# A new order of the same work in an attention and expert kernel on one core

## The chip, the core and the metric

The kernel runs on one core of one Trainium2 chip. A core has TensorE (PE in the profile, with PEld for its loads of stationary operands), VectorE (DVE), ScalarE (ACT), GpSimd (POOL) and SyncE (SP, which only issues transfers). The metric is the device time of one execution in microseconds (us); lower is better.

## The reference

The inputs q, k and v have 8 batch entries, 8 heads, 576 positions and 64 numbers a head, in float32. The expert part has a gate vector of 512, w1 (512 x 1024), w2 (1024 x 512) and a capacity of 128.

```python
q_rot, k_rot = (rotate(q), rotate(k))            # rotary embedding, halves of 32
scores = 1/sqrt(D) * np.matmul(q_rot, k_rot.transpose(0, 1, 3, 2))
attn = np.exp(scores - scores.max(-1)); attn /= attn.sum(-1) + 1e-09
x = matmul(attn, v)  -> (B, S, 512)
scores = np.einsum('bsd,d->bs', x, w_gate)       # expert part, for each batch entry
top_idx = np.argpartition(-scores[b], capacity)[:capacity]
ye = np.maximum(x[b, top_idx] @ w1, 0.0) @ w2
out[b, top_idx] = x[b, top_idx] + sigmoid(scores[b, top_idx])[:, None] * ye
```

## The kernel before, in words

Four heads make a group; there are two groups for each batch entry and 16 in all. A group's four heads are two pairs, so pairs are numbered 0 to 31, and pairs 2g and 2g+1 belong to group g. For a pair, q and k come from memory as two planes (the numbers, and the numbers with their halves swapped) into the tiles q_in and k_in, of which four each are used in turn; `rotate` multiplies both planes by a table (tabk) and adds them. Pair 0 is cut in column pieces and its rotation is written for VectorE, the pieces of q after the first for VectorE or GpSimd (`both`). Pairs 1 to 3 may also go to either; pair 1 is multiplied plane by plane. All later pairs are rotated on GpSimd.

`attend` then works through nine units of 64 rows (`units`). A unit multiplies q by k for one pair or for both pairs ("scores") into banks of PSUM. There are eight banks and a unit takes two for each of its pairs. In groups 0 and 1 the first 6 and 3 units are done pair by pair (`APART`). A unit's scores leave their banks in one of two ways, chosen by the table `DRAINS` (one letter for group, pair and unit): "V" means that VectorE copies and finds the row's extreme in one instruction; "S" means that ScalarE copies and VectorE finds the extreme from the copy. ScalarE then takes the exponential with the row sum, and VectorE transposes blocks (`turn`, STREAM_TRANSPOSE). `value` multiplies the transposed rows (tile prob) by v (tile vt) in six steps of 96 multiplications into four banks, copies the result (ot), transposes it on TensorE and scales it by the row sums into x; `half_done` stores x and multiplies it by the gate vector on GpSimd (tile prod). After every second group `route` ranks the positions of a batch entry, `chosen` gathers the chosen rows back from memory (GpSimd, tile xe), and `experts_of` runs w1, relu (ht) and w2 and scatters the rows.

The order of the work is a table. Every `op` gets a number in the order in which the program makes it, and `LINES` lists for each engine the numbers in the order in which that engine shall run them, two characters each; an op that several engines could run goes to the one whose line lists it. `Order.run` plays these lines with assumed costs (`SWITCH` and `RESTART` for TensorE when it changes between its three kinds of work or begins after a wait, the two lines on `wire` and `lasts` for transfers), and gets from that one order over all engines and the PSUM banks of each op. The instructions are written out in that order; on the chip an engine runs its own in that sequence and waits on semaphores. The assumed costs are no instructions: they reach the chip only through the order and the banks. A transfer marked `alone` waits until the one three before it has landed (`DEPTH = 3`). Because ops are written through one helper, all instructions show line L243; rows are told apart by tile names.

Of the kernel before, what the change touches and what calls it, by code (L numbers as in the profile page):

```python
# [33 lines left out]
010Q0H1e151n0Y1w1D1s1i1J0U100L19352Z2P3h3a2U312K1T3o1U3v1V1W3B1X1Y3I5a5g5G2521235m5z5L5t5W5R3R3S3T3U3V3W6V6Q6+417c433-75  # L34
7o7v7h7B6566674B68696a4I6f6h9a8Y936j4L7L9h7M7N7O9m7P7Q9x9s9D7Z4O9J7V7X4SaC4TaPaI4VaW8n4Wb1b79T9Ubd9V9Wbk9X9Ybpc+cNa18ucU
d3a54Ya38x4Z4+da4-bAbBdfbCbDdkbEbFdvdpepbObKbM8AeveC8E8FeIdGeOdHeUdIdJdKdLeZgxdUdQccdS8H8If4fagDcj8K8LgIcm8MgO8Ng-gVfkfl
h5fmhbfnfofphgiacpfwfyfuimighrithshtiyhuhvhwiKiEiQhBhFhDctcukmiVkhfYcwcxkskzg3czkFcAkKcBg6kQcCj4j5kWj6j7j8j9l0lVjijgjeg9
# [6 lines left out]
7n71787r7A747b7u6b6c7D6g9e9b7F9094977T8Z99924Q6p8-969l9j9g9p9d9o7R7S9A6r9z9E9r4P9w7+9C9I9u9GaD854U9NaQaJ87aMaT9LaLa+aX4X
b49-b8aHaFaOb0bhb6b3beaVaZaSbgbj9+9ZbsbobacObccRcVbmd7brcQbud4a4a6d6bId2d0d9abcTcZdccXaddjdhde8CdobHbGdydmdqafduesds8Bez
dxdAbUeFewdO8GbWeJeBeEbYereReHeNeLeQeueyeWeYeTdNdMe+f1gAdVdTf0f38Jd+f5gCf7f9gHgzfefcgJcrgFgSgLgPh0gNgUgRgWh4e0h2h6g+hagY
hfhde2h8fqfrhhibhjhlcqiniqfEihidfGijifilipivixisiBhyhxiLiHiAiDiJiGhGcvhLkniWhNkriNiPiSiUcyktkAi+iYjckwkpklkjkHkCkLkTkykJ
kNkPkEkZkvkSkYkVk-jajbl2lWl4gahPmcgbmlmim8mgm0jom7mkmemrmam2lYjsmtl+m4mnmymqlhlgmClnmwmEmBo4gfmImHo8ocmKo3oeoagio6okowoq
# [1029 lines left out]
```

## Time and profile before

| | us |
|---|---|
| median of 3 runs (lowest, highest) | 521.37 (519.64, 522.71) |
| the profiled execution's own time | 518.34 |
| its span, first to last instruction | 516.6 |
| PE busy in the span | 484.8 (94%) |
| DVE busy | 449.5 (87%) |
| ACT busy | 392.0 (76%) |
| POOL busy | 349.9 (68%) |

The profiled execution lies below all three timed runs, so differences are worked out against it and then applied to the median. The 1.7 us between its span and its own time lie outside the first and last instruction. Busy time of PE counts modelled ends of pipelined matmuls; where matmuls follow one another, the distance between starts is the safer number.

### The profile page before, as it was taken

The page shows a single profiled execution, that of the slowest core. Times are in us where ns is not written, and L with a number is a line of the kernel's source. Part 1 is how long each engine was busy: PE and PEld are TensorE (multiplying, and loading weights), DVE is VectorE, ACT ScalarE, POOL GpSimd, SP SyncE. Part 2 cuts the span into 40 slices and gives each one's busy share as a digit, 9 for nine tenths or more (in the row PEclk, how much of TensorE's full clock was granted, in tenths as well). Part 3 has the DMA queues.
Part 4 walks back from the last instruction along what each step waited for, and adds up shares of the span by engine and source line. Part 5 has one row for each costly group of instructions (what it writes and reads, how often), then busy time and mean ns, then how long its engine had stood idle before and what let it go on. Part 6 is the DMA issues. An engine that isn't in the chain of part 4 may idle for free.

```text
span 516.6 us, 18965 instructions
## 1 busy us (share of the span) xinstructions
PE 484.8 (94%) x7988; PEld 303.3 (59%) x7988; DVE 449.5 (87%) x781; ACT 392.0 (76%) x1040; POOL 349.9 (68%) x304
## 2 busy tenths in 40 slices
PE   8679978799999999999999999999999998999995
PEld 7345545455665456664567555674658455666872
DVE  6899999999999999989989998999949998993710
ACT  1598999998889989987778868977579967981100
POOL 2977498699884997749797796947796588114110
PEclk9798999999999999999999999999999999999998
DMA  8776556565554737235651746460642543132210
GB/s 293 233 258 201 159 176 203 177 194 159 152 173 127 202 114 217 82 120 167 206 163 61 204 129 222 132 221 16 184 137 86 161 138 110 50 86 64 88 42 20
DMA packets 47381, 76.53 MB, mean 148 GB/s; under 512 B 4928, under 2 KB 28224, under 8 KB 47296
## 3 DMA queue, kind: packets, MB, share of 16 engines
q1 hardware_dynamic: 45472, 70.54, 45.0%
q0 software_dynamic: 1280, 4.20, 2.4%
q8 instruction: 63, 1.03, 0.9%
q10 hardware_dynamic: 544, 0.59, 0.4%
q14 instruction: 22, 0.18, 0.1%
HBM read 63.77 MB, written 11.53 MB: 146 GB/s over the span
## 4 chain that ended last, share of the span: by engine, by line
PE 42%; POOL 10%; issue 9%; ACT 6%; DVE 4%; DMA 3%; POOLq 0%; ACTq 0%; DVEq 0%; SPq 0%
PE banks L243 42%; POOL k_in L243 3%; POOL q_in L243 3%; ACT prob L243 3%; POOL prod L243 2%; DVE prob L243 2%; ACT ot L243 2%; DVE nm L243 1%; DMA q_in<-q_dram 1%; DMA k_in<-k_dram 1%; ACT prod L243 1%; DVE past L243 0%; POOL xe L243 0%; POOL out_dram L243 0%; ACT ht L243 0%
## 5 line engine op out<-in xcount | busy, mean ns | idle before, releaser
L243 ACT ACTIVATE prob<-prob,nm 128x576 f32<-128x576 f32 x288 | 220.7, 771 | 25.8 <-DVE prob L243 14.3
L243 PE MATMUL banks<-k_in,q_in 64*64 64x288 f32 x2304 | 181.9, 420 | 22.6 <-ACT prob L243 5.1
L243 DVE STREAM_TRANSPOSE prob<-prob 128x2304 f32<-128x2304 f32 (+2 forms) x98 | 187.1, 1926 | 3.7 <-ACT prob L243 3.5
L243 PE MATMUL banks<-prob,vt 32*64 32x288 f32 x4608 | 151.6, 405 | 0.0
L243 PEld LDWEIGHTS banks<-k_in,q_in 64*64 64x64 f32 x2304 | 86.8, 134 | 106.7 <-ACT prob L243 23.0
L243 PEld LDWEIGHTS banks<-prob,vt 32*64 32x64 f32 x4608 | 98.3, 132 | 50.0 <-issue 14.1
L243 DVE TENSOR_SCALAR_CACHE_REDUCE prob<-banks 128x576 f32<-128x576 f32 x142 | 103.9, 746 | 13.5 <-PE banks L243 10.5
L243 ACT ACTIVATE prob<-banks 128x576 f32<-128x576 f32 x146 | 92.2, 653 | 28.9 <-PE banks L243 28.4
L243 DVE TENSOR_REDUCE nm<-prob 128x1 f32<-128x576 f32 x146 | 103.6, 738 | 3.4 <-ACT prob L243 3.1
L243 POOL TENSOR_TENSOR q_in<-q_in,tabk 128x1152 f32<-128x1152 f32 (+1 forms) x32 | 82.3, 2578 | 14.8 <-DMA q_in<-q_dram 14.5
L243 POOL TENSOR_TENSOR k_in<-k_in,tabk 128x1152 f32<-128x1152 f32 (+1 forms) x31 | 81.5, 2630 | 10.8 <-DMA k_in<-k_dram 7.9
L243 POOL TENSOR_TENSOR prod<-x,wg 128x512 f32<-128x512 f32 (+1 forms) x45 | 49.5, 1099 | 30.4 <-DVE x L243 13.9
L243 PE MATMUL banks<-xt,w1t 128*128 128x128 f32 x512 | 61.5, 277 | 0.1
L243 PEld LDWEIGHTS banks<-xt,w1t 128*128 128x128 f32 x512 | 58.9, 192 | 4.2 <-issue 2.3
L243 PE MATMUL banks<-w2t,ht 128*128 128x512 f32 x128 | 60.9, 607 | 0.3 <-ACT ht L243 0.3
L243 ACT ACTIVATION_READ_ACCUMULATOR prob<-prob,nm 128x1 f32 x288 | 56.1, 195 | 0.0
L243 POOL TENSOR_SCALAR sel<-slots,rank 128x128 bf16<-128x128 bf16 x35 | 20.6, 608 | 40.0 <-DVE rank L243 40.0
L243 POOL TENSOR_TENSOR k_in<-k_in 128x576 f32<-128x576 f32 x31 | 44.5, 1437 | 0.8
L243 POOL TENSOR_TENSOR q_in<-q_in 128x576 f32<-128x576 f32 x30 | 42.6, 1425 | 0.4
L243 PEld LDWEIGHTS banks<-w2t,ht 128*128 128x128 f32 x128 | 22.3, 189 | 23.9 <-issue 23.5
L243 ACT ACTIVATE prod<-prod 128x256 f32<-128x256 f32 (+1 forms) x54 | 22.0, 411 | 8.5 <-POOL prod L243 8.4
L243 POOL DMA_INDIRECT out_dram<-xe,idx x8 | 8.3, 1040 | 29.6 <-DVE xe L243 28.8
(69 smaller groups left out, 284.4 us busy)
## 6 DMA issues: line engine op xcount, KB each, us to landing
k_in<-k_dram SPq DMA_DIRECT2D x64, 288.0 KB, 3.6
vt<-v_dram SPq DMA_DIRECT2D x96, 192.0 KB, 3.1
q_in<-q_dram SPq DMA_DIRECT2D x62, 288.0 KB, 3.4
out_dram<-x SPq DMA_DIRECT2D x32, 256.0 KB, 2.8
w2t<-w_dram SPq DMA_DIRECT2D x8, 256.0 KB, 4.0
w1t<-w_dram SPq DMA_DIRECT2D x8, 256.0 KB, 3.4
out_dram<-x SPq DMA_DIRECT2D x16, 64.0 KB, 2.6
tabk<-rope_dram ACTq DMA_DIRECT2D x2, 288.0 KB, 4.2
```

The source lines that it names most:

```text
L243: i = made(*args, **kwargs)
```

## The change

Three assumed costs change, and the two tables are made anew: `LINES` for all five engines, and `DRAINS`.

```diff
-RESTART = (70.0, 130.0, 70.0)
+RESTART = (70.0, 130.0, 130.0)
...
-                            wire = max(wire, begin + takes) + o.moved / 350.0
-                            lasts = max(wire - begin + 1700.0, takes + 1400.0 + o.moved / 137.0)
+                            wire = max(wire, begin + takes) + o.moved / 300.0
+                            lasts = max(wire - begin + 2200.0, takes + 1900.0 + o.moved / 137.0)
...
-            on = any_of(n) if both else {"DVE": dve(n)} if first else {"POOL": pool(n)}
+            on = {"DVE": dve(n) if first else dve(n, 1, 700.0), "POOL": pool(n)} if both else {"DVE": dve(n)} if first else {"POOL": pool(n)}
...
-        ("VVVVVSSSS", "SVSSSVSVS"),
-        ("SSVSSSSSV", "SVSSSSVSS"),
+        ("VVVVVVVVV", "VSVVVSSSV"),
+        ("SSSSSSSVV", "SSSVSVVSS"),
...
-0B0D0E0F2G2H2I2E2J2F2C2D521-545356555857593Z6O6I2a6P6J6K6M6L6N2c8Q6d2e8S484a8U4c8T8R8W8X4C8VaA4Kay6oaB6qau4Navaw6saxaz82
+0B0z0C0D0F0E0G2C2A2D2B2y2w2z2x1V514Z4+4X4Y4-50526H6I246D6E6F6G3S266B6C8I28668J8M8K418N43458O4v8P8Latan4Dao6h7L4Gar6jasau
```

The first: a unit of scores that begins behind a wait is assumed to cost 130 ns and not 70. The second: a transfer is assumed to run at a lower rate and to last 500 ns longer. The third: a rotation instruction of pairs 1 to 3 is assumed to take 700 ns longer on VectorE. No instruction changes its operands, but some change their engine: in the whole program 148 pieces of scores leave PSUM by "V" and 140 by "S" (before: 142 and 146), four of the sixteen relus go from ScalarE to VectorE, and four scalings of x from VectorE to ScalarE.

Three places of the new order follow. The first is GpSimd at the start of the program; k_in1 and q_in1 are pair 1, q_in0 is pair 0, the tiles with 2 and 3 are pairs 2 and 3 (group 1). A row with tabk is a multiplication, one without it a sum. Before:

```order
L243 TENSOR_TENSOR k_in1_79<-k_in1_79,tabk_69 128x576
L243 TENSOR_TENSOR k_in1_79<-k_in1_79 128x576
L243 TENSOR_TENSOR q_in1_75<-q_in1_75,tabk_69 128x576 x2
L243 TENSOR_TENSOR k_in3_81<-k_in3_81,tabk_69 128x1152
L243 TENSOR_TENSOR k_in3_81<-k_in3_81 128x576
L243 TENSOR_TENSOR q_in3_77<-q_in3_77,tabk_69 128x1152
```

Now:

```order
L243 TENSOR_TENSOR k_in1_79<-k_in1_79,tabk_69 128x576
L243 TENSOR_TENSOR q_in0_74<-q_in0_74,tabk_69 128x2x192
L243 TENSOR_TENSOR k_in1_79<-k_in1_79,tabk_69 128x576
L243 TENSOR_TENSOR k_in1_79<-k_in1_79 128x576
L243 TENSOR_TENSOR q_in1_75<-q_in1_75,tabk_69 128x576 x2
L243 TENSOR_TENSOR q_in1_75<-q_in1_75 128x576
L243 TENSOR_TENSOR q_in3_77<-q_in3_77,tabk_69 128x1152
L243 TENSOR_TENSOR k_in3_81<-k_in3_81,tabk_69 128x1152
```

GpSimd has taken over the other half of k_in1's multiplication, one multiplication of q_in0 and the sum of q_in1; pairs 2 and 3 come after these. VectorE in the same stretch, before (prob0 is group 0; TENSOR_SCALAR drains a unit by "V", TENSOR_REDUCE belongs to "S"):

```order
L243 TENSOR_SCALAR prob0_86,nm0_93<-banks_63 128x576
L243 STREAM_TRANSPOSE prob0_86<-prob0_86 128x576
L243 TENSOR_SCALAR prob0_86,nm0_93<-banks_63 128x576
L243 TENSOR_REDUCE nm0_93<-prob0_86 128x1
L243 TENSOR_TENSOR q_in1_75<-q_in1_75 128x576
L243 STREAM_TRANSPOSE prob0_86<-prob0_86 128x576 x3
L243 TENSOR_REDUCE nm0_93<-prob0_86 128x1
L243 TENSOR_SCALAR prob0_86,nm0_93<-banks_63 128x576
```

Now:

```order
L243 TENSOR_SCALAR prob0_86,nm0_93<-banks_63 128x576 x2
L243 TENSOR_TENSOR q_in0_74<-q_in0_74 128x192
L243 TENSOR_SCALAR prob0_86,nm0_93<-banks_63 128x576 x2
L243 STREAM_TRANSPOSE prob0_86<-prob0_86 128x576
L243 TENSOR_SCALAR prob0_86,nm0_93<-banks_63 128x576 x2
L243 STREAM_TRANSPOSE prob0_86<-prob0_86 128x576 x5
L243 TENSOR_SCALAR prob0_86,nm0_93<-banks_63 128x576
```

The sum of q_in1, which stood between a reduction and three transposes, is gone from VectorE, and the last sum of q_in0 (128x192) stands behind two drains and waits for GpSimd's multiplication.

The second place is TensorE in the expert part of batch entry 3 (minus, past: counting the rank; w2t, ht: the second expert product; tok, sel: the index; k_in, q_in: scores). Before:

```order
L243 MATMUL banks<-minus,past_115 128x1
L243 MATMUL banks<-w2t,ht_101 128x512 x2
L243 MATMUL banks<-k_in_78,q_in_74 64x288
L243 MATMUL banks<-k_in_79,q_in_75 64x288
L243 MATMUL banks<-k_in_78,q_in_74 64x288
L243 MATMUL banks<-k_in_79,q_in_75 64x288
L243 MATMUL banks<-k_in_78,q_in_74 64x288
L243 MATMUL banks<-k_in_79,q_in_75 64x288
L243 MATMUL banks<-k_in_78,q_in_74 64x288
L243 MATMUL banks<-k_in_79,q_in_75 64x288
L243 MATMUL banks<-w2t,ht_101 128x512 x4
L243 LDWEIGHTS sel_107
```

Now:

```order
L243 LDWEIGHTS past_115
L243 MATMUL banks<-minus,past_115 128x1
L243 MATMUL banks<-w2t,ht_101 128x512 x6
L243 LDWEIGHTS sel_107
L243 MATMUL banks<-tok_110,sel_107 128x5
L243 LDWEIGHTS sel_107
```

The unit of scores no longer stands between two runs of the expert product; it stands in a run of five units (40 multiplications) ahead of the counting. Over the whole program the runs of scores, of values and of other work fall from 168 to 157. From the first use of gathered rows on, runs of scores fall from 65 to 58 and runs of value products from 33 to 32, and the longest runs of scores there are five units where they were four.

The third place is GpSimd around the gather of batch entry 5 (out_5; rs, sums: the guard on the row sums; prod, x, wg: products with the gate vector). Before:

```order
L243 DMA xe1_103<-out_5_dram,idx1_109 128x512
L243 TENSOR_SCALAR rs1_96<-sums1_92 64x2x5 x2
L243 TENSOR_SCALAR rs1_96<-sums1_92 64x2x4 x2
L243 TENSOR_TENSOR q_in3_77<-q_in3_77,tabk_69 128x1152
L243 TENSOR_TENSOR q_in2_76<-q_in2_76,tabk_69 128x1152
L243 TENSOR_TENSOR q_in3_77<-q_in3_77 128x576
L243 TENSOR_TENSOR q_in2_76<-q_in2_76 128x576
L243 TENSOR_TENSOR k_in3_81<-k_in3_81,tabk_69 128x1152
L243 TENSOR_TENSOR k_in3_81<-k_in3_81 128x576
L243 TENSOR_TENSOR prod0_97<-x0_89,wg_70 64x256
L243 TENSOR_TENSOR k_in2_80<-k_in2_80,tabk_69 128x1152
L243 TENSOR_TENSOR k_in2_80<-k_in2_80 128x576
```

Now:

```order
L243 DMA xe1_103<-out_5_dram,idx1_109 128x512
L243 TENSOR_TENSOR prod0_97<-x0_89,wg_70 128x512
L243 TENSOR_TENSOR q_in3_77<-q_in3_77,tabk_69 128x1152
L243 TENSOR_TENSOR prod0_97<-x0_89,wg_70 128x512
L243 TENSOR_TENSOR k_in3_81<-k_in3_81,tabk_69 128x1152
L243 TENSOR_TENSOR q_in3_77<-q_in3_77 128x576
L243 TENSOR_TENSOR k_in3_81<-k_in3_81 128x576
L243 TENSOR_TENSOR prod0_97<-x0_89,wg_70 64x256
L243 TENSOR_TENSOR q_in2_76<-q_in2_76,tabk_69 128x1152
L243 TENSOR_TENSOR k_in2_80<-k_in2_80,tabk_69 128x1152
L243 TENSOR_TENSOR k_in2_80<-k_in2_80 128x576
L243 TENSOR_TENSOR q_in2_76<-q_in2_76 128x576
```

The guard on the sums is gone to ScalarE, and two large products of x now stand ahead of and between the multiplications of pairs held in the tiles 2 and 3.

## Rows read from the trace of the kernel before

**Rows 1.** Page, part 1: busy us (share of the span) and instructions, by engine.

```profile
PE 484.8 (94%) x7988; PEld 303.3 (59%) x7988; DVE 449.5 (87%) x781; ACT 392.0 (76%) x1040; POOL 349.9 (68%) x304
```

**Rows 2.** Stretch, length; busy PE, PEld, DVE, ACT, POOL; granted clock; DMA share, GB/s.

```profile
0.00:20.00 20.00, 14.03 (x94) 11.25 (x94) 16.06 (x41) 5.94 (x12) 10.82 (x18) 0.97 0.84 278
20.00:40.00 20.00, 16.66 (x142) 9.17 (x146) 17.83 (x29) 16.53 (x38) 15.79 (x8) 0.84 0.78 242
40.00:60.00 20.00, 19.59 (x400) 11.12 (x396) 18.91 (x29) 18.54 (x43) 14.41 (x11) 0.93 0.51 153
60.00:120.00 60.00, 49.42 (x1017) 29.57 (x1012) 59.65 (x92) 59.07 (x173) 48.81 (x41) 1.00 0.66 198
120.00:480.00 360.00, 354.14 (x6163) 220.07 (x6156) 327.02 (x551) 289.30 (x772) 254.97 (x219) 1.00 0.46 137
```

**Rows 3.** Timeline of the start: begin, length, instruction, idle time before it.

```profile
10.39 0.75 DVE L243 TENSOR_TENSOR k_in<-k_in,tabk 128x576 f32<-128x576 f32 x1
10.56 1.85 POOL L243 TENSOR_TENSOR k_in<-k_in,tabk 128x576 f32<-128x576 f32 x1 [7.94 <-DMA k_in<-k_dram]
...
16.72 2.62 POOL L243 TENSOR_TENSOR k_in<-k_in,tabk 128x1152 f32<-128x1152 f32 x1
16.79 3.16 DVE L243 TENSOR_TENSOR q_in<-q_in 128x576 f32<-128x576 f32 x1
...
20.01 14.58 PE L243 MATMUL banks<-k_in,q_in 64*64 64x288 f32 x118 [4.40 <-DVE q_in L243]
...
22.94 0.75 DVE L243 TENSOR_REDUCE nm<-prob 128x1 f32<-128x576 f32 x1 [0.98 <-ACT prob L243]
...
36.56 0.74 DVE L243 TENSOR_SCALAR_CACHE_REDUCE prob<-banks 128x576 f32<-128x576 f32 x1
...
37.46 1.20 PE L243 MATMUL banks<-k_in,q_in 64*64 64x288 f32 x16 [2.87 <-POOL k_in L243]
```

**Rows 4.** Groups by line and shape: count, busy us, mean ns of one.

```profile
L243 DVE TENSOR_SCALAR_CACHE_REDUCE prob<-banks 128x576 f32<-128x576 f32 x142 | 103.9, 746 | 13.5 <-PE banks L243 10.5 <-ACT prod L243 1.5 <-ACT prob L243 0.5
L243 DVE TENSOR_REDUCE nm<-prob 128x1 f32<-128x576 f32 x146 | 103.6, 738 | 3.4 <-ACT prob L243 3.1
...
L243 ACT ACTIVATE prob<-banks 128x576 f32<-128x576 f32 x146 | 92.2, 653 | 28.9 <-PE banks L243 28.4
...
L243 POOL TENSOR_TENSOR k_in<-k_in,tabk 128x1152 f32<-128x1152 f32 x30 | 79.6, 2656 | 2.9 <-PE banks L243 2.7
...
L243 POOL TENSOR_TENSOR q_in<-q_in 128x576 f32<-128x576 f32 x30 | 42.6, 1425 | 0.4
L243 POOL TENSOR_TENSOR prod<-x,wg 128x512 f32<-128x512 f32 x30 | 38.5, 1283 | 26.0 <-DVE x L243 13.9 <-ACT prod L243 5.7 <-DMA k_in<-k_dram 3.2
...
L243 POOL TENSOR_TENSOR q_in<-q_in,tabk 128x576 f32<-128x576 f32 x2 | 2.8, 1404 | 0.0
```

**Rows 5.** Timeline of TensorE alone, later in the run.

```profile
414.66 1.71 PE L243 MATMUL banks<-prob,vt 32*64 32x288 f32 x48
416.30 1.20 PE L243 MATMUL banks<-k_in,q_in 64*64 64x288 f32 x16
417.43 3.17 PE L243 MATMUL banks<-prob,vt 32*64 32x288 f32 x96
420.53 1.20 PE L243 MATMUL banks<-k_in,q_in 64*64 64x288 f32 x16
421.66 2.68 PE L243 MATMUL banks<-prob,vt 32*64 32x288 f32 x80
```

**Rows 6.** Timeline around the gather of batch entry 5.

```profile
411.14 1.11 POOL L243 DMA_INDIRECT xe<-out_dram,idx  x1 [0.28 <-POOL idx L243]
...
415.64 0.86 POOL L243 TENSOR_SCALAR rs<-sums 64x10 f32<-64x10 f32 x3 [2.82 <-DMA xe<-out_dram,idx]
...
433.57 2.17 PE L243 MATMUL banks<-k_in,q_in 64*64 64x288 f32 x32 [1.94 <-POOL k_in L243]
```

**Rows 7.** Waits: us in total, times, longest.

```profile
POOL prod L243 <- DVE x L243: 13.9, 6, 4.8
```

More of the change, by code (lines that the diff above doesn't have):

```diff
@@ L26 @@
 BLOCK, FETCH = 256, 3950.0
-RESTART = (70.0, 130.0, 70.0)
+RESTART = (70.0, 130.0, 130.0)
 LINES = {
     "PE": """
[L34 to L37, printed above, removed]
@@ L44 @@
[L44 to L48, printed above, removed]
@@ new lines @@
+d0cWd69Y9+4R4S8p4T4UbrbsbtdcbubvbwdndhbFbBehbD8seneu8w8xezdyeFdzdAeLdBdCdDeQgodIc3dK8zdM8AeXf1gu8Ccagz8D8EcdgE8FgLgRfbgX
+fcfdh1fefffgh6i1fnfpcgflidi8hihjikhkhliphmhniuiAiGhuhwckhscliMkdk8cnfPcokjkpkvkBfWcqkIcrcsctfZiXiYkOiZi+i-j0kUlOj5g0j7j9
+m4mal+lUl3l4mhl5l6mml7l8mrldlfg4g5mwnUo4n+jzlhg7g8onobohotoAjGgagbgcjJgdmHmIoFmJmKmLmMpzjMmRmVmToQpGoRpMoSq3oToUoVq8pTpZ
+p2njjQp0jRnqo+jTrHjUrNqentjWqkjXrTjYjZr+qus5qvsbqwqxqyqzsgslqGqEnwqIsrtdtjnAnBtptwnDtCr6nEtPtJsCtVsDsEt+sFsGsHrdnGsMnHsQ
+rgsOudueufuguhuinIrjurupunrnnJuCrqrouJrtuMrrrurvuPrwuTuWuUuXuZu+u-v0""",
+    "ACT": """
@@ new lines @@
+h9chihiei7i4iciaimijigfxioithphoixiriBiwiziDiJhvhtiNkghCiRiIiLiFiPcpkkkqkykchEkFkCkikakfkAkxkmkuhGkJkHkEg2kokskPkLkTkNkR
+j2j1kXlPg1kZkWm5mbmel-lXjfm3mdm9m1mgmlm7lWlRmjjjmql9lalZlTlgmvmtg6momznVo5o8n-linZmyo3g9ooocokoxo1ognXmBomojoumPlnoeo7oa
+oEoCosoqoGozoIowjOoKmOmNpApDjNoYmWpJpQpNm-pCpLpIpSpPpFoWoXqbpWpYp+q5q7pVq2q0p1p3o-rIjVrQqaqfqdrMrPnyqhqjqoqmrUp8rKrSrXs2
+r-rZrWs8qCsas4s1s7sfsdqBqApcsisosknxsstgsqsnqOtitmtfnCsutqttqStzswtstDtGtvtlnFtStBtMtItytUtotFt-tRtOtLtZtXsIsJu3u1sNrlsY
+ujs+usrpuRrs""",
+    "DVE": """
@@ new lines @@
+iyiEfOiCiUiHhxcmiKiQkekhiOk9kbfUfRfVfTfSknktiWklkwfXkziVkMkDkrkGk+cuf+j4l0kSkKkQg3k-l1kVkYlSj6j8jam8l2m2lQmclVm0lYmfmkm6
+mijhmDlcmpjymnmEmsmulemCmxnYmFjEo2nWjDjBjFjCo0orofoiopo6mAo9jHoloBodoDmGovjKoyoLgemQoMoJoHoNjPoOoPpEmSmUlppHpKoZlrpBq4pR
+q6pOn1n3q9qcnipUpXq1npnonnnmp-nlqpnrqqrLjSqrrRrOqiqgnuqnrJqlnzqsqtrVj+rYsxs6s9s3s0pascqDsesyszshsjsmqHqFqJspsvsttethtksA
+qQtnu4tur5txtrsBrar8r9rcrbtAtQtHtKtTu6tYtWtNtEu5u7u2sLu8u0u9reuaubucrhsPumsRsWukrkuquormuvuwuxuuutuBuInKuFuHuGuEuKuLuNuQ
+uSrxuVuYv1""",
@@ L473, in attention_moe_kernel @@
     DRAINS = (
-        ("VVVVVSSSS", "SVSSSVSVS"),
-        ("SSVSSSSSV", "SVSSSSVSS"),
-        ("VVSVSVVVS", "SSSSSVSVV"),
-        ("VVSSVSSVV", "VVSSVSSSV"),
-        ("SSSVVVVSV", "SSSVSVSVV"),
-        ("SSSSVSSVV", "VSSSSVSVS"),
-        ("SSVSVVVSV", "SVVSVVVVS"),
-        ("VSVSVVSSV", "SSSVSVSVV"),
-        ("VVSSSSSVS", "SVVSVVVVV"),
-        ("SSSVVVSVS", "VVSVSSVVV"),
-        ("VSSSVSVVV", "VVSVVVSSV"),
-        ("SSVSSVVVV", "VVSVSSVSS"),
-        ("VSSSSSVVV", "SVVVVVVVV"),
-        ("SSSSVVVSS", "VVSVSSSSV"),
-        ("VVVSVVSVS", "SVSSVSVSV"),
-        ("SVSSSVVSV", "VSSVSSSVV"),
+        ("VVVVVVVVV", "VSVVVSSSV"),
+        ("SSSSSSSVV", "SSSVSVVSS"),
+        ("SSVSVVSSV", "SVSSVSVVV"),
+        ("VVVSVVSSV", "VVSVSSSSV"),
+        ("SSSVVSVSS", "SVSSVSVVV"),
+        ("VVSSVSSSV", "VVSSSVSVS"),
+        ("SSSVSSVSV", "VVVSVVVVS"),
+        ("VSVVVVSVV", "SSVSSVSSV"),
+        ("VVVSVVVVS", "SVVSSSSVS"),
+        ("SVSVVVSVS", "SVSVVSVSV"),
+        ("VVSSVSSSV", "VSVVSSVVS"),
+        ("SVSSSVVVV", "VSVVSVVVS"),
+        ("SSSSVSSVS", "VVSVSVSVV"),
+        ("SVSVSVVSV", "SSSSVVSVV"),
+        ("SVSSVVVVS", "VSSSSVVSV"),
+        ("VVSVSVVVS", "SSSSSSSVV"),
     )
```

46 lines of the change are left out of this document (20 added, 26 removed).

## The prediction, made before the changed kernel was run

> **What bounds the kernel now.** I read the page's busy shares first, then the table of busy time by stretch, then the timeline of the start and of one later place, the groups by shape, and the list of waits. The shares alone say "TensorE" (94%, [rows 1]), and that is an average over two different regimes. In the first 120 us TensorE is idle for 5.97 + 3.34 + 0.41 + 10.58 = 20.3 us; from 120 to 480 us it is idle for 5.9 us out of 360 [rows 2]. In the late stretch a saving on TensorE itself counts almost in full. In the early stretch it is VectorE and ScalarE that are full: 59.65 and 59.07 us busy out of 60 between 60 and 120 us, and VectorE has only 2.17 and 1.09 us of idle time in the two stretches before that [rows 2].
>
> The start has one large hole. VectorE's sum for q_in1 begins at 16.79 us, 0.07 us after a GpSimd multiplication that lasts until 19.34, and takes 3.16 us; TensorE then begins pair 1's scores at 20.01 after an idle time of 4.40 us which the row puts down to that sum [rows 3]. In the stretch that follows, the granted clock is 0.84: of the two levels, 1.2 and 2.4 GHz, the lower held for about a third of it. The second hole, 2.87 us before 37.46, is put down to a GpSimd rotation; but pair 2 is what that unit reads, and a VectorE drain ends at 37.30 [rows 3], so I read it as a wait for a bank, that is, for VectorE.
>
> **The change, part by part.** The assumed costs are not executed; only the order, the choice of engine and the banks count.
>
> *Start.* Three rotation instructions leave VectorE: the sum of q_in1 (3.16 us), one multiplication of k_in1 (0.75 us, [rows 3]) and one of q_in0 (no row of its own; 384 columns against 576, so about two thirds of 0.75, 0.5 us). Up to group 3's last transpose VectorE has nine more "V" drains at 746 ns and eight fewer reductions at 738 ns [rows 4], one of the nine belonging to the next group; that is even. So VectorE loses 3.16 + 0.75 + 0.5 = 4.4 us, and ScalarE ten copies of 653 ns, 6.5 us, up to its last exponential of group 3.
>
> Little of this comes out at the end, because pair 1's scores are now released by GpSimd. Its chain before them is two multiplications of k_in1, one of q_in0, the sum, two multiplications and the sum of q_in1: four times 1.40, twice 1.43 [rows 4], and 0.9 for q_in0 (a third of the 2.66 of 1152 columns; it has no row, and lies between nothing and 1.40), 9.4 us. It begins when the first half of k_in1 has landed: VectorE used one half at 10.39 without a wait and GpSimd got the other at 10.56 [rows 3]; in the new order of SyncE's queue k_in1's first half is the fifth transfer, not the sixth, so between 9.0 and 10.4. Pair 1 is ready between 18.4 and 19.8 us, on average 0.9 us before 20.01. VectorE waits there too, and so cannot spend the rest of its 4.4 us before that point.
>
> Behind that point VectorE has about the work that it had. What it can still win is its idle time up to 60 us, 2.17 + 1.09 less the 0.98 just before 22.94, that is 2.3 us, most of it in waits for ScalarE or for TensorE's first units [rows 2, 3]; ScalarE's missing copies shorten the former. I take half, 1.1 us. The sum for the start is 0.9 + 1.1 = 2.0 us. Bounds: nothing, if the gate does not move and the idle time comes back elsewhere; 0.9 + 2.3 = 3.2 us, if all is won. GpSimd must now do pairs 2 and 3 later: from 19.1 on four multiplications at 2.66 and four sums at 1.43 end at 35.5 us, when TensorE wants pair 2 at 37.46 less the gain. At 2.0 us of gain the two meet; a greater gain would be stopped here.
>
> *Longer runs on TensorE.* From the first gathered rows on there are seven fewer runs of scores, one fewer of values and six fewer of the rest. A run of 48 value records takes 1.64 us to the next start and one of 96 takes 3.10, so 48 more cost 1.46 and a run costs 0.18 us beyond its records. A run of 16 scores takes 1.13 us (416.30 to 417.43) [rows 5]; its own records are an estimate from value rows: scores move as many columns, half as many records in the same time, 16 x 2 x 30.4 ns = 0.97, so 0.16 us a run beyond its records. A unit that is no longer inserted therefore saves 0.16 + 0.18 = 0.34 us; seven save 2.4 us. In the expert product the return is not priced by a row, and I use the same. This lies in the stretch where TensorE is idle for 1.6% of the time, so it is on the path. Against it, longer runs of scores need banks sooner: with eight banks two paired units are in flight, and the third waits for a drain (0.65 to 0.75 us, [rows 4]). The longest runs grow from four to five units, in two places; I take 0.2 us for each off the sum and come to 2.0 us. Bounds: 1.0, if each run of five loses 0.75 us, and 2.4.
>
> *Transfers.* They have the same sizes; q_in1's halves are the 11th and 12th on SyncE's queue instead of the 9th and 11th. GpSimd reaches them some 5 us after k_in1, so I cost this at nothing; if the cover is gone, what is late is pair 1 again, and the 0.9 us go.
>
> *Sum.* 2.0 + 2.0 = 4.0 us, 518.3 - 4.0 = 514.3 against the profiled execution's own time (span 516.6 and 1.7 around it). That execution was 3.0 us faster than the median of the timed runs, 521.4, which is what a new median has to be held against: 521.4 - 4.0 = 517.4 us.
>
> *A rule weighed.* VectorE's 3.16 us against 0.75 for a multiplication of the same size is a wait for GpSimd's whole instruction: 19.34 - 16.79 = 2.55 us, then 0.6 of work [rows 3]. GpSimd's 1.85 us against 1.40 in the same kind of instruction, beside a VectorE rotation, is the other direction [rows 3, 4]. The Trainium skill, page "SBUF — State Buffer", section "Who interferes with whom", says that a VectorE instruction with two inputs in SBUF contends with a GpSimd instruction that reads SBUF, and that the later of the two stands still until the first is done; the trace agrees. This rule speaks against one line of the change, in the second rival.
>
> **The rivals.** *Nothing left over.* The start's gain goes unspent (GpSimd's chain ends at 19.8 and pair 2 meets the gate) and runs of five wait for banks: between 0.2 + 1.0 and 2.0 us remain, 520.2 to 519.4; I put 519.6. For it: VectorE is full to 120 us with hardly less to do behind the gate. Against it: ScalarE's 6.5 us.
>
> *The wait returns one instruction earlier.* In the new order VectorE's last sum of q_in0 waits for GpSimd's multiplication of it, and GpSimd goes straight on with k_in1. If that multiplication starts first, the sum stands for its 1.40 us [rows 4] with five drains behind it. VectorE's 12 drains and transposes of pair 0 then end after pair 1's first unit, and 1.4 us of the gain are lost: 521.4 - 2.6 = 518.8.
>
> *Slower: products ahead of the rotations.* At the gather of batch entry 5 TensorE already waited 1.94 us for pair 2's k, 22.43 us after the gather began [rows 6]. Now GpSimd does there 1.11 for the gather, two products at 1.28, a smaller one (0.64, half), four multiplications at 2.66 and four sums at 1.43: 20.6 us [rows 4, 6], 1.8 less, if no product waits. Both large ones need x scaled by ScalarE, and everything behind them waits with them. A product's wait for x was 13.9 us in six cases, 2.3 on average and 4.8 at most [rows 7]. With one wait of each kind the rotations are 7.1 - 1.8 = 5.3 us later, all of it idle TensorE; after the 4.40 us hole at the start the clock cost about half of 6.4 us at the lower level (0.16 of 20 us is 3.2, [rows 2]). That makes 5.3 + 3.2 - 4.0 = 4.5 us more, 525.9. It decides from 1.8 us of waiting on; slower than the bound below it is from 1.8 + 4.0 + 2.6 - 3.2 = 5.2 us.
>
> **How the numbers follow.** A median of this kernel cannot be told from no change within 0.5%, 2.6 us: faster means below 518.8, slower above 524.0. The forecast has a chance of 0.48, with a range of its own from 515.8 (3.2 + 2.4) to 518.8; nothing left over 0.26; the wait returned 0.08, on the border and counted as the same; slower 0.18. That gives 0.48 faster, 0.34 the same, 0.18 slower. For 8 in 10 the range goes from 513.0, below the forecast's own for what chance brings in a median (the three runs lie 3.1 us apart), up to 525.0, which takes in the milder part of the slower case.
>
> **What would show it.** Right: TensorE's first hole shorter than 4.40 us and released by GpSimd; no VectorE sum of 3 us; the hole before 37.46 ending at 35 to 36; idle time up to 120 us of 17 to 19 us; from 120 to 480 us the same 6 us of idle and a span of that part shorter by 2. Wrong: the x-products at batch entry 5 with waits over 2 us and TensorE idle behind them, a granted clock below 1.00 after 120 us, waits of score runs for drains, or a VectorE sum of q_in0 near 1.7 us.

## The result, and the profile after

The changed kernel took 515.0 us in the median (514.23 to 515.82, four runs) beside 520.5 us for the kernel before: a ratio of 0.989, 95% interval [0.985, 0.994]. In a second comparison, kernel beside kernel on one chip, it was 510.05 against 517.75 us, 0.986 [0.984, 0.989]. The forecast of 4.0 us less was right in direction and low in size: 5.5 and 7.7 us were measured. The profiled execution took 514.23 us against 518.34, 4.1 us less. That agrees with the forecast's sum by accident: its two terms were both too small, and this one execution lost some 3.7 us in another way (below).

The page of the changed kernel, part 1 (answers to [rows 1]):

```profile
PE 481.6 (94%) x7988; PEld 306.0 (60%) x7988; DVE 446.8 (87%) x786; ACT 389.1 (76%) x1046; POOL 355.0 (69%) x311
```

The stretches of the changed kernel (columns as in [rows 2], to which they answer):

```profile
0.00:20.00 20.00, 15.04 (x109) 11.87 (x113) 14.27 (x40) 5.87 (x12) 12.14 (x20) 1.00 0.85 289
20.00:40.00 20.00, 16.47 (x166) 8.94 (x158) 20.00 (x37) 17.14 (x40) 18.89 (x14) 1.00 0.75 240
40.00:60.00 20.00, 18.55 (x408) 10.40 (x406) 20.00 (x31) 18.93 (x50) 15.85 (x8) 1.00 0.65 197
60.00:120.00 60.00, 51.25 (x1087) 30.39 (x1089) 59.57 (x100) 58.40 (x173) 52.55 (x50) 1.00 0.59 172
120.00:480.00 360.00, 353.51 (x6080) 225.90 (x6069) 324.86 (x553) 287.38 (x773) 251.21 (x218) 1.00 0.46 141
```

VectorE has no idle time at all from 20 to 60 us, where it had 3.26 before; the granted clock, 0.97, 0.84 and 0.93 before, is 1.00 (2.4 GHz throughout). TensorE's idle time is 18.7 us up to 120 us (20.3 before) and 6.5 us from there to 480 (5.9 before).

The start of the changed kernel, as a timeline (answers to [rows 3]):

```profile
9.23 1.82 DVE L243 TENSOR_TENSOR q_in<-q_in 128x128 f32<-128x128 f32 x2
9.24 1.53 POOL L243 TENSOR_TENSOR k_in<-k_in,tabk 128x576 f32<-128x576 f32 x1 [6.63 <-DMA q_in<-q_dram]
...
11.10 6.04 PE L243 MATMUL banks<-k_in,q_in 64*64 64x288 f32 x48 [1.90 <-DVE q_in L243]
12.34 0.76 DVE L243 TENSOR_SCALAR_CACHE_REDUCE prob<-banks 128x576 f32<-128x576 f32 x1 [1.29 <-PE banks L243]
13.99 0.97 DVE L243 TENSOR_TENSOR q_in<-q_in 128x192 f32<-128x192 f32 x1
...
17.68 1.40 POOL L243 TENSOR_TENSOR q_in<-q_in 128x576 f32<-128x576 f32 x1
...
18.55 3.41 DVE L243 STREAM_TRANSPOSE prob<-prob 128x576 f32<-128x576 f32 x5
18.78 2.52 PE L243 MATMUL banks<-k_in,q_in 64*64 64x288 f32 x32 [1.64 <-DVE prob L243]
21.88 0.72 DVE L243 TENSOR_SCALAR_CACHE_REDUCE prob<-banks 128x576 f32<-128x576 f32 x1
...
35.03 5.13 PE L243 MATMUL banks<-k_in,q_in 64*64 64x288 f32 x56 [1.84 <-POOL k_in L243]
```

The 3.16 us sum is gone. Another one stands instead: of the two sums at 9.23 the second, 256 columns wide, begins just after GpSimd's multiplication of k_in1 and lasts until 11.05, and the sum at 13.99 takes 0.97 us for 192 columns (0.35 before). The first scores start at 11.10, later than before (8.26). But from 18.55 on VectorE works without a break into pair 1's first drain at 21.88.

VectorE's account up to group 3's first value product shows where the start's gain is. The busy time of the core's engines in these two stretches, the kernel before first and the changed kernel second (columns as above):

```profile
0.00:118.05 118.05, 97.75 (x1588) 59.94 (x1588) 110.51 (x184) 98.67 (x261) 87.89 (x77) 0.96 0.68 211
```

```profile
0.00:113.81 113.81, 95.25 (x1605) 57.80 (x1605) 107.68 (x191) 95.35 (x256) 94.50 (x81) 1.00 0.67 208
```

VectorE works 110.51 - 107.68 = 2.83 us less and idles 7.54 - 6.13 = 1.41 us less. Together that is the whole 4.24 us by which that value product comes earlier. Such an account closes for every engine (ScalarE: 3.32 us less work, 0.92 less idle time), so by itself it names no cause; that VectorE is the one has to come from the runs below.

From group 3's last value product to the last product of all it is 381.4 us before and 380.6 in this execution, so almost nothing. (A group's values are 288 records, six steps of 48; a step is 24 multiplications, not 96.) Five runs of value products in it lasted 0.7 us longer than their records. One of them, and the same run in the second profile of the changed kernel:

```profile
356.97 3.90 PE L243 MATMUL banks<-prob,vt 32*64 32x288 f32 x96
```

```profile
354.16 3.17 PE L243 MATMUL banks<-prob,vt 32*64 32x288 f32 x96
```

In that second profile the late part took 376.9 us, 4.5 less than before.

### The profile page after: what moved, and what is told of

Its sections match the earlier page's. It is cut to its first block, busy times and chain, and to the rows that moved or that the text cites. A ratio compares the mean times of both kernels' runs of the same rounds, so it can differ in the third digit from the quotient of the medians.

```text
span 512.3 us, 18990 instructions
## 1 busy us (share of the span) xinstructions
PE 481.6 (94%) x7988; PEld 306.0 (60%) x7988; DVE 446.8 (87%) x786; ACT 389.1 (76%) x1046; POOL 355.0 (69%) x311
## 4 chain that ended last, share of the span: by engine, by line
PE 67%; ACT 13%; DVE 7%; issue 6%; POOL 5%; DMA 1%; SPq 1%; POOLq 0%; DVEq 0%; ACTq 0%
PE banks L243 67%; ACT prob L243 8%; DVE prob L243 4%; ACT ot L243 3%; POOL k_in L243 2%; POOL q_in L243 2%; DVE nm L243 2%; ACT x L243 2%; DMA q_in<-q_dram 1%; SPq L243 1%; DVE past L243 0%; ACT prod L243 0%; POOLq L1073 0%; POOL xe L243 0%; POOL out_dram L243 0%
## 5 line engine op out<-in xcount | busy, mean ns | idle before, releaser
L243 PE MATMUL banks<-k_in,q_in 64*64 64x288 f32 x2304 | 175.4, 413 | 20.1 <-DVE prob L243 6.1
L243 PE MATMUL banks<-prob,vt 32*64 32x288 f32 x4608 | 154.7, 405 | 2.4 <-DVE xe L243 1.5
L243 PEld LDWEIGHTS banks<-k_in,q_in 64*64 64x64 f32 x2304 | 83.9, 132 | 99.9 <-issue 20.7
L243 PEld LDWEIGHTS banks<-prob,vt 32*64 32x64 f32 x4608 | 103.1, 132 | 50.5 <-issue 14.3
L243 DVE TENSOR_SCALAR_CACHE_REDUCE prob<-banks 128x576 f32<-128x576 f32 x148 | 108.4, 745 | 20.8 <-PE banks L243 18.6
L243 ACT ACTIVATE prob<-banks 128x576 f32<-128x576 f32 x140 | 88.6, 654 | 29.7 <-PE banks L243 28.9
L243 DVE TENSOR_REDUCE nm<-prob 128x1 f32<-128x576 f32 x140 | 100.1, 739 | 1.6 <-ACT prob L243 1.6
L243 POOL TENSOR_TENSOR q_in<-q_in,tabk 128x1152 f32<-128x1152 f32 (+2 forms) x33 | 83.4, 2533 | 5.5 <-DMA q_in<-q_dram 4.6
L243 ACT ACTIVATION_READ_ACCUMULATOR prob<-prob,nm 128x1 f32 x288 | 58.4, 203 | 0.0
L243 ACT ACTIVATE x<-banks,rs 128x64 f32<-128x64 f32 (+1 forms) x144 | 31.2, 338 | 2.4 <-PE banks L243 2.2
```

Of the source, the lines that this page charges most:

```text
L243: i = made(*args, **kwargs)
```

## The experiments

Theories. V: up to group 3's first value product VectorE is the bound, and what it is spared there comes out. G (the prediction's): pair 1's release is the gate, and the rest stays unspent. C: the lower granted clock behind the hole of 4.40 us is what costs. For each run the table gives the time of group 3's first value product, VectorE's busy and idle time until then, and the time from group 3's last value product to the end, all from the profiles; and the ratio of the times to the kernel before on the same chip.

| run | first value product, us | VectorE busy + idle | late part | ratio [95%] |
|---|---|---|---|---|
| before | 118.05 | 110.51 + 7.54 | 381.4 | 1 |
| changed | 113.81 | 107.68 + 6.13 | 380.6 | 0.989 [0.985, 0.994] |
| before, q_in1's sum on GpSimd | 115.07 | 107.08 + 7.99 | 381.3 | 0.994 [0.991, 0.996] |
| changed, that sum on VectorE | 117.39 | 110.33 + 7.06 | 376.3 | 0.993 [0.991, 0.996] |
| before, hole filled | 114.97 | 107.55 + 7.42 | 384.4 | 0.996 [0.994, 0.999] |
| changed, VectorE filled early | 119.71 | 110.12 + 9.59 | 377.0 | 1.001 [0.998, 1.004] |
| changed, again | 114.02 | 107.68 + 6.34 | 376.9 | 0.986 [0.984, 0.989] |
| changed, 14 breaks | 115.62 | 108.23 + 7.39 | 404.1 | 1.035 [1.031, 1.038] |
| changed, other start | 116.26 | 107.69 + 8.57 | 376.6 | 0.990 [0.987, 0.994] |
| changed, two edits | 115.95 | 107.44 + 8.51 | 381.2 | 0.998 [0.996, 1.000] |
| sum on GpSimd, hole filled | 116.08 | 107.21 + 8.87 | 384.4 | 0.995 [0.993, 0.997] |
| sum on GpSimd, again | 117.16 | 107.59 + 9.57 | 383.1 | 0.995 [0.993, 0.997] |
| changed, VectorE filled late | 115.30 | 107.78 + 7.52 | 380.8 | 0.992 [0.989, 0.995] |
| before, again | 119.15 | 110.16 + 8.99 | 382.5 | 1.001 [0.998, 1.003] |

Single profiles of one order differ by the granted clock, and this limits what one row of the table can say. TensorE's scores ahead of group 2's values, in the kernel before and in the same kernel run again:

```profile
96.58 3.61 PE L243 MATMUL banks<-k_in,q_in 64*64 64x288 f32 x48 [0.89 <-ACT prob L243]
```

```profile
96.51 4.83 PE L243 MATMUL banks<-k_in,q_in 64*64 64x288 f32 x48 [0.89 <-ACT prob L243]
```

From 84 us up to here TensorE's rows of the two agree within 0.1 us, waits included. Then the clock of the second was at 1.2 GHz from 96.9 to 100.3 us, and its group 3 began 1.10 us later. In the same way the changed kernel run again and the one filled late, which is the same up to 180 us, part where the latter's clock was at 1.2 GHz, from 69.0 to 72.5 us, and its group 3 began 1.28 us later. So 1 to 2 us between two rows can be the clock of one execution; the ratios come from many.

**One sum moved.** On VectorE's and GpSimd's lines of the kernel before:

```diff
 VectorE:  reduction of u5
-          sum of q_in1
           transposes u4, u5, u3
 GpSimd:   multiplications of q_in1, both halves
+          sum of q_in1
           multiplication of pair 3's k
```

> The kernel before with one instruction moved: the sum of q_in1 goes from VectorE to GpSimd, behind its two multiplications. VectorE loses 3.16 us there, GpSimd gains some 1.4 and makes pair 1 ready at about 16.7 + 1.4 = 18.2 us instead of 20.0. Theory V (VectorE bounds the kernel up to group 3's first value product, so each microsecond taken off it comes out at the end): 3.2 us faster. Theory G (that of the prediction: the release of pair 1's scores is the gate, and what VectorE is spared beyond it stays unspent): 1.8 us faster. Theory C (the hole of 4.40 us on TensorE costs mainly by the lower granted clock behind it, 0.07 and 0.16 of 20 us each, 4.6 us): 4 us faster or more, with a granted clock of 1.00 from 20 to 60 us.

Measured: 515.53 against 518.18 us. Pair 1's scores started at 17.88 instead of 20.01, 2.1 us earlier; VectorE had 3.43 us less to do and 0.45 more idle time, and group 3 began 2.98 us earlier:

```profile
17.88 6.52 PE L243 MATMUL banks<-k_in,q_in 64*64 64x288 f32 x60 [2.69 <-POOL q_in L243]
```

V is met, G is not. The gain did not need the clock, which was still 0.95 and 0.88 in the first two stretches; what a higher one would add, the run does not say. Nor did it need fewer copies on ScalarE, whose work stayed the same (98.55 against 98.67 us).

**The same sum moved back.**

```diff
 VectorE:  drain u4
+          sum of q_in1
           transposes u0, u2, u3, u4, u1
 GpSimd:   multiplications of q_in1, both halves
-          sum of q_in1
           multiplication of pair 3's q
```

> The changed kernel with that one instruction moved back: the sum of q_in1 on VectorE again, behind the sixth drain of pair 0. It will meet GpSimd's multiplication for pair 3 (17.7 to 20.3 us) and end near 20.9. Theory V: VectorE loses 0.6 us of work and some 1.8 us of waiting, 2.4 us slower. Theory G: pair 1 is ready at 20.9 instead of 19.1, 1.8 us slower. Theory C: the hole grows from 1.64 to about 3.8 us, the granted clock falls behind it, 4 us slower or more.

Measured: 514.7 against 518.18 us. Group 3 began 3.4 us later than with the change (117.39 against 114.02), of which VectorE's work is 2.65. The ratio lies 0.4 to 0.7% above those of the changed kernel, 2 to 4 us. V's 2.4 and C's 4 both fit the time, and the account does not part them: 2.2 of the 3.4 us are there when group 0's values are under way (48 us), and 1.0 comes at group 2, where the clock was at 1.2 GHz from 92.5 to 96.0 us. ScalarE kept its lighter work (95.68 us) and won at most 0.7 us by it (117.39 against 118.05 in the kernel before).

**The hole filled, in the kernel before.**

```diff
 TensorE:  pair 0, units u1 u0 u4 u3 u5 u2
+          20 identity products into a free bank
           both pairs, unit u6
```

> The kernel before with 20 more identity products (40 records, some 4 us) on TensorE in its hole between pair 0's last single unit and pair 1's scores, into a bank that nothing reads. The hole is filled and the clock should stay up; VectorE's work and the release of pair 1 stay as they were. Theory V: no change, within 0.5 us, whatever the clock does from 20 to 60 us. Theory G: no change. Theory C: 3 to 4.6 us faster.

Measured: 516.29 against 518.18 us. All three theories said something else, and the timeline told why. VectorE's and GpSimd's instructions at that place:

```profile
16.61 0.75 DVE L243 TENSOR_TENSOR q_in<-q_in 128x576 f32<-128x576 f32 x1
...
17.13 2.72 POOL L243 TENSOR_TENSOR k_in<-k_in,tabk 128x1152 f32<-128x1152 f32 x1 [0.60 <-DMA k_in<-k_dram]
...
19.81 4.52 PE L243 MATMUL banks<-k_in,q_in 64*64 64x288 f32 x54
```

In this execution GpSimd's multiplication waited 0.60 us for its transfer, VectorE's sum came first and took 0.75 us instead of 3.16. Pair 1's scores began at 19.81, as good as before (20.01), with the same gate; and still group 3 began 3.08 us earlier, with 2.96 us less work on VectorE. This separates V from G better than any planned run: the gate stood, the work went, and the time came out at group 3. At the end of this execution it did not: the late part is 3.0 us longer than before (384.4 against 381.4) and the profiled time the same (518.31 against 518.34), since behind a wait around the gather of batch entry 5 the clock was at 1.2 GHz from 430.3 to 437.1 us. On C the start says nothing, since two things differ; a share of the 3.08 us may be the clock's.

**VectorE filled early.** Five fillings of a tile that nothing reads, 0.54 us each:

```diff
+ for _ in range(5): op({"DVE": dve(S)}, lambda: nc.vector.memset(spare, 0.0))
  (on VectorE's line behind the drains and reductions at 39 to 82 us)
```

> The changed kernel with five more VectorE instructions that fill a tile of 128 x 576 values which nothing reads, spread over 42 to 84 us, about 0.55 us each, 2.7 us in all. Theory V: 2.7 us slower, in full. Theory G: at most 0.5 us slower, since pair 1's release is long past. Theory C: no change, the clock stays at 1.00.

Measured: 517.44 against 518.18 us, so nearly the whole gain of the change is lost. Group 3 began 5.7 us later than in the changed kernel (119.71 against 114.02): 2.4 us of work, 3.3 us of new idle time. G falls. V has the right sign and half the size; the other half comes from a chain. C's premise did not hold: the clock was at 1.2 GHz from 70.8 to 77.7 us. TensorE's timeline around group 1's values, in this run and in the changed kernel's second profile, and VectorE's next drain in this run:

```profile
70.92 2.20 PE L243 MATMUL banks<-k_in,q_in 64*64 64x288 f32 x16 [1.21 <-DVE prob L243]
74.85 10.34 PE L243 MATMUL banks<-prob,vt 32*64 32x288 f32 x288 [1.73 <-DVE prob L243]
85.12 1.20 PE L243 MATMUL banks<-k_in,q_in 64*64 64x288 f32 x16
```

```profile
69.41 1.20 PE L243 MATMUL banks<-k_in,q_in 64*64 64x288 f32 x16 [0.98 <-DVE prob L243]
70.54 8.99 PE L243 MATMUL banks<-prob,vt 32*64 32x288 f32 x288
```

```profile
86.39 0.76 DVE L243 TENSOR_SCALAR_CACHE_REDUCE prob<-banks 128x576 f32<-128x576 f32 x1 [3.45 <-PE banks L243]
```

Scores and values are late for VectorE's sake, and then slow: 2.20 us instead of 1.20 and 10.34 instead of 8.99 at the lower clock, 2.35 us in all. The next unit of scores stands behind all 288 value records, and VectorE, which had been full, waits 3.45 us for it. How much of the 5.7 us would be left at the higher clock was not measured.

**The changed kernel again.**

> The changed kernel once more, beside the others of this group. In its first profile five runs of value products stood still for about 0.7 us each (3.6 us against 0.4 to 1.3 in the other profiles). Theory R (these stalls belong to an execution, not to the order): a second profile has at most two of them, and from group 3's last value product to the last product it takes 376.4 to 377.5 us, as in the two runs that share its late order, instead of 380.6. Theory O (the new order brings them): again four or five, and 380 to 381 us. The time: 5 to 6 us faster than before.

Measured: 510.05 against 517.75 us; late part 376.9 us, at most two longer value runs instead of five. R is met and O falls, with one correction that the last four runs made: these pauses go with the chip that a kernel runs on, as far as these profiles show (last section). The 7.7 us are more than expected.

**Fourteen breaks.** At 14 places from group 4 on, in TensorE's line:

```diff
-          other, other, scores, scores
+          other, scores, other, scores
```

> The changed kernel with 14 more breaks between TensorE's runs, all from group 4's scores on: at 14 places the last operation of an expert product or transposition and the first paired unit of scores behind it change places, so that 14 runs of scores and 14 of the rest are added. Theory S (the prediction's price, 0.34 us for a unit that stands by itself): 14 x 0.34 = 4.8 us slower. Theory N (a break costs nothing by itself, and the late gain came from waits that went away): within 1 us.

Measured: 536.42 against 510.05 us for the changed kernel on the same chip, 26 us slower; both theories were far off. The late part has 73 runs of scores instead of 59. TensorE's idle time from 120 to 480 us went from 6.2 to 25.8 us:

```profile
120.00:480.00 360.00, 334.21 (x5695) 206.42 (x5686) 312.72 (x523) 279.75 (x748) 243.67 (x201) 0.99 0.45 135
```

Half of it stands behind the two names under which scores leave their banks. TensorE's waits for them in this stretch (total us, times, longest), which in the changed kernel come to 0.8 us:

```profile
PE banks L243 <- ACT prob L243: 9.3, 12, 1.6
PE banks L243 <- DVE prob L243: 3.1, 5, 1.6
```

So, as far as these releasers tell, a unit put one operation earlier meets banks that are not free. Some 3 us more are two value runs at 1.2 GHz (from 265.0 and 377.6 us on), 1.5 and 1.7 us too long. The run does not give the bare price of a break, but its records and those of the changed kernel do: a record of scores is followed after 0.333 us by one of another kind and after 0.225 by the next group of scores, the first group of a run takes 0.273 instead of 0.225, and an expert product or transposition is followed by scores 0.093 later than by its own kind. That is 0.25 us for a unit that stands by itself, where the prediction had 0.34. The Trainium skill, page "TensorEngine Tiling (Array Packing)", section "Key Properties", says that a change of tiling mode drains TensorE; the three kinds here stand in three modes (32x64, 64x64 and 128x128 in the rows), and the trace agrees, with this price.

**Another start.**

```diff
 GpSimd:   k_in1 first half, q_in0's last mult.,
+          q_in0's last sum,
           k_in1 second half, ...
 TensorE:  pair 0: u5 u2 u3 u0 u4 u1
-          both pairs: u6 u7   pair 1: u0 ...   both: u8 ...
+          u6 u7 u8   pair 1: u6 u7 u0 u1 u3 u2 u8 u5 u4
```

> The changed kernel with another start: GpSimd's first multiplication of k_in1 waits for VectorE's sum of q_in0's middle piece, so that this sum is not held up; the last sum of q_in0 goes to GpSimd; all nine units of pair 0 stand ahead of pair 1's; two transfers stand one place earlier. Theory V: VectorE is spared 1.2 + 0.97 us of sums and 1.3 us of waiting for its first drain, 2 to 3 us faster than the changed kernel. Theory G: GpSimd's chain, which began at 9.24, begins at about 10 and has one sum more; pairs 1 to 3 are ready 1.3 us later and the kernel is 0.5 to 1.3 us slower than the changed one.

Measured: 511.89 us, 1.8 slower than the changed kernel. One part of the edit did not reach the chip: the wait on GpSimd was entered for the order only, so its multiplication began at 9.12 and the middle sum stood as long as before. What was left is a GpSimd chain longer by one sum, and VectorE with 2.2 us more idle time, 1.39 of it at 39.7 us, where it waits for scores that run at 1.2 GHz (36.8 to 40.2 us; 56 records in 6.77 us, 5.13 in the changed kernel). In this profile 1.6 us are thus the clock's. But executions at a mean clock of 1.00 took 511.29 and 511.54 us, against 510.31 of the changed kernel, so that G's size is about right here.

**Two edits.**

```diff
 GpSimd:   q_in0's last mult.
+          q_in0's last sum
 TensorE:  expert and token products
+          group 10, unit u7 (scores)
           group 9, first value product
```

> The changed kernel with two edits: the last sum of q_in0 (0.97 us on VectorE with its wait) goes to GpSimd, and group 10's seventh unit of scores stands ahead of group 9's first value product, where TensorE waited 1.45 us for VectorE's expert sum. Theory V and a late stretch in which a wait of TensorE counts in full: 0.9 + 1.1 = 2.0 us faster than the changed kernel. Theory G: pair 1 is ready 0.5 us later, and only the late microsecond is won, 0.5 us faster.

Measured: 516.34 us, 6.3 slower than the changed kernel. Both edits lost. VectorE was spared 0.24 us net and idled 2.2 us more up to group 3, about half of it at group 2, where the clock was at 1.2 GHz (91.3 to 94.7 us). And the value product that was to follow the scores at once:

```profile
295.52 1.20 PE L243 MATMUL banks<-k_in,q_in 64*64 64x288 f32 x16
300.44 4.15 PE L243 MATMUL banks<-prob,vt 32*64 32x288 f32 x64 [3.72 <-DVE prob L243]
```

It needs four banks that now hold the scores, and waits 3.72 us instead of 1.45. Behind this wait the clock was at 1.2 GHz from 299.5 to 306.3 us, and the group's values lasted 2.9 us longer than their records; that is more than the wait itself cost. Neither of these two versions beats the changed kernel.

**The filled hole without the lottery.** The kernel with the sum on GpSimd, plus:

```diff
 TensorE:  pair 0, units u1 u0 u4 u3 u5 u2
+          11 identity products into a free bank
           both pairs, unit u6
```

> The kernel before with the sum of q_in1 on GpSimd, and 11 more identity products (22 records, 2.6 us) that fill the hole of 2.69 us which TensorE then has ahead of pair 1's scores. In the run without them the granted clock was 0.95, 0.88 and 1.00 from 0 to 20, 20 to 40 and 40 to 60 us. No wait of VectorE differs between the two. Theory V: the same time as without the filling, within 0.5 us, and the first value product of group 3 at the same 115.1 us, whatever the clock. Theory C: the clock stays at 1.00 and 0.05 + 0.12 of 20 us, 3.4 us, come out.

**and its base again, without an edit:**

> The kernel before with the sum of q_in1 on GpSimd, once more, as the base for the one with the filled hole. Theory V: the first value product of group 3 again at 115.1 us, 3 us ahead of the profile of before, and some 381.3 us from group 3's last value product to the end, as in before. Theory G: a median no more than 1.8 us below before.

Measured: 518.10 with the filling and 518.08 without, on the same chip. The first two stretches without and with it:

```profile
0.00:20.00 20.00, 15.90 (x121) 12.84 (x124) 15.09 (x43) 6.67 (x14) 11.06 (x18) 0.99 0.82 278
20.00:40.00 20.00, 16.89 (x136) 9.22 (x132) 18.93 (x29) 18.48 (x43) 17.62 (x13) 0.84 0.82 254
```

```profile
0.00:20.00 20.00, 18.34 (x146) 14.61 (x146) 15.08 (x42) 6.58 (x14) 10.99 (x18) 1.00 0.83 277
20.00:40.00 20.00, 15.97 (x144) 8.88 (x140) 19.41 (x30) 19.39 (x45) 18.74 (x14) 0.91 0.83 248
```

The clock is higher by 0.01 and 0.07 of 20 us, the hole is closed, and the medians are the same. The profiles are not. The filled kernel is 0.88 us ahead at group 1's first value product (70.45 against 71.33) and 1.08 at group 3's, which V did not expect, and loses that around the gather of batch entry 5. The scores that wait there for GpSimd's rotation of k, without and with the filling:

```profile
434.33 2.17 PE L243 MATMUL banks<-k_in,q_in 64*64 64x288 f32 x32 [2.06 <-POOL k_in L243]
```

```profile
433.50 3.12 PE L243 MATMUL banks<-k_in,q_in 64*64 64x288 f32 x32 [2.39 <-POOL k_in L243]
```

Behind the longer wait the clock was at 1.2 GHz from 434.6 to 438.0 us; the scores and the 32 products behind them (4.51 us against 3.84) lost 1.6 us. In the other filled kernel the wait was 2.70 us, the clock low for twice as long, and the same rows lost 2.9. So C's 3.4 us did not come, and the clock is not the main cost of the first hole; but some 0.9 us there may be its share, and late in the kernel, where TensorE is full, it costs time.

The base alone gives V a second chip: at group 1 it is 2.98 us ahead of the kernel before (71.33 against 74.31), on the first pair of profiles 2.94. At group 3 it is only 1.99 ahead (117.16 against 119.15), and 2.1 later than expected: its clock was at 1.2 GHz from 91.1 to 97.9 us. Its median is 2.4 us lower; G's 1.8 lies inside that interval.

**VectorE filled late.** The same five fillings, behind drains and a reduction of groups 6 to 13.

```diff
+ for _ in range(5): op({"DVE": dve(S)}, lambda: nc.vector.memset(spare, 0.0))
  (on VectorE's line behind unit u4's drain or reduction of groups 6, 7, 9, 11, 13)
```

> The changed kernel with the same five VectorE fillings of 0.54 us as in the run with them between 42 and 84 us, but now in groups 6, 7, 9, 11 and 13 (from about 180 to 400 us), where VectorE has about a tenth of idle time. Theory V, which makes VectorE the bound up to group 3's first value product only: within 0.5 us of the changed kernel, where the early ones made group 3 5 us later. Theory W (every engine's order is so tight that anything put in is paid in full or more, wherever it stands): 2.7 us slower or more.

Measured: 516.1 us, ratio 0.992 [0.9891, 0.9952], whose interval overlaps the first of the changed kernel and just misses the second (up to 0.9890); by the time alone it is undecided. The late part, with the five longer value runs, took 380.8 us, and 380.6 in the profile of the changed kernel that also had them: 0.2 us for 2.7 us of work. W falls, V holds: late in the kernel VectorE has room.

**The kernel before again.**

> The kernel before, once more. In its first profile VectorE's sum of q_in1 began 0.07 us after a GpSimd multiplication and took 3.16 us; in the run with the filled hole the multiplication began 0.5 us later, waiting for its transfer, and the same sum took 0.75 us. Theory L (which of the two starts first is settled anew in each execution): the sum takes either about 3.2 or about 0.75 us, and the first value product of group 3 stands at about 118.0 with the one and 115.0 with the other; the single times are spread over some 5 us, as they were (515 to 521.5). Theory F (the order alone fixes it): 3.16 us again.

Measured: 521.23 us. The place of the long sum:

```profile
17.54 3.16 DVE L243 TENSOR_TENSOR q_in<-q_in 128x576 f32<-128x576 f32 x1
```

GpSimd's multiplication began at 17.48, 0.06 us ahead of it, as in the first profile (0.07). Two of two profiles of the unmodified kernel have the long sum; the short one was seen only where a transfer came late. F has the better of it; that other executions win the race is left open.

## Why the prediction was right, and where its steps were not

*The start* was put at 2.0 us, at most 3.2. It gave 4.0 to 4.2, outside the bounds. The step that failed is "VectorE waits there too, and so cannot spend the rest of its 4.4 us before that point". The gate itself moved as forecast: GpSimd's sum for pair 1 ends at 19.08, 0.9 us before 20.01, where the forecast had 0.9. But VectorE does not wait at it, because it has transposes of pair 0 in hand until 21.88, and from there on it is never out of work. The run with the filled hole shows the same from the other side. What should have been added up is VectorE's account, 2.8 us less work and 1.4 less idle time. About 3.0 us are the one sum (shown by moving it, on two chips); of the rest, some 0.9 us may be the clock, for which the sum of the start had no term, and the parts were not separated. The stop at pair 2, where a gain above 2.0 us was to end, did not hold either: GpSimd releases that unit at 35.03, 2.4 us earlier than 37.46, and VectorE has work in hand meanwhile.

*VectorE's removed work* was put at 4.4 us; 2.8 came out, since 1.2 + 0.6 us returned as standing time of two sums of q_in0. This is the second rival's mechanism, one instruction earlier than it was looked for, and dearer than its 1.4 us. Its time, 518.8, was wrong all the same, as it was subtracted from a gain that was too small.

*Longer runs on TensorE* were put at 2.0 us. The late part became 4.5 us shorter where no pauses disturb it (381.4 to 376.9; three other runs with this order and without the pauses lie at 376.3 to 377.0, two of them on a chip where the order before, with the sum moved, took 381.3). On the chip with pauses in both orders it was 382.5 and, with the late fillings, 380.8, only 1.7 us. The parts, from the records: runs of scores 66 to 59 and other runs 40 to 34, at 0.25 us some 1.8 us, close to the forecast; the hole of 1.94 us at batch entry 5 is gone; one unit of scores, 1.0 us, had moved ahead of the point from which I count; against that, 1.45 us of a new wait ahead of group 9's values. These make 3.3 of the 4.5; the rest is spread over waits below 0.5 us and was not settled. The 14 breaks show that the order's other effect, which banks a unit finds free, can be far larger than the price of a switch; in the sum it stood only as 0.4 us for two runs of five.

*The slower rival* did not come. The gather of batch entry 5 in the changed kernel (answers to [rows 6]):

```profile
405.19 1.12 POOL L243 DMA_INDIRECT xe<-out_dram,idx  x1 [0.74 <-POOL idx L243]
...
408.33 2.65 POOL L243 TENSOR_TENSOR q_in<-q_in,tabk 128x1152 f32<-128x1152 f32 x1 [0.70 <-DMA q_in<-q_dram]
...
425.92 1.41 POOL L243 TENSOR_TENSOR q_in<-q_in 128x576 f32<-128x576 f32 x1
```

No product waits for x there. The chain from the gather to the last sum is as long as before (22.1 us against 22.4), but the gather starts 6.0 us earlier, and the scores that need its end only 4.7 us earlier. The rival's term for the clock behind a longer wait at this place, 3.2 us, is near the 2.9 us that the kernel with the filled hole lost there.

*What would show it.* Right: the hole before pair 1 shorter than 4.40, no sum of 3 us, the hole at 37.46 ending at 35.03, 18.7 us of idle time up to 120 us, 6.5 us from 120 to 480. Wrong: the hole is released by VectorE's bank, not by GpSimd; the sign given for a failure, a sum near 1.7 us, appeared (1.62) without the failure.

## What to carry to other kernels

Where an engine is full from one end of a stretch to the other, add up its work and its idle time on both sides of a change; a gate elsewhere costs only as much as it leaves that engine without work. Removing work there paid nearly in full (3.43 us gave 2.98); putting 2.4 us in cost 5.7, when a unit of scores slipped behind a block of values and the clock fell. An order of many buffers in flight can be worth more by which buffer is free when than by how often it switches: 14 small exchanges cost 26 us. And where the clock can fall, read it beside every row before a difference of a microsecond is put down to an edit.
